# An attention and mixture-of-experts kernel: blocks of one expert's 128 rows become doubles, singles and mixed blocks of two experts' 64 rows each

## The chip, the cores and the metric

The kernel runs on one core of one Trainium2 chip. The metric is the device time of one execution in microseconds (us); shorter is better. All timed runs that are compared here were marked fast, which means within 1.5% of the fastest run of the same kernel; the one single look is named where it comes up.

Trace abbreviations: PE is TensorE (matrix products), PEld its loading of weights, DVE is VectorE, ACT ScalarE, POOL GpSimd and SP SyncE, which here queues the transfers of weights. The granted clock is the share of TensorE's full clock that it was given, 1.00 at most. A "pass" is one matrix-product instruction of the trace; a float32 product shows as two passes, a transpose as one (in the trace of the kernel before a block's layer 1 of 32 products shows 64, its four transposes 4). "L1024" is a line of the kernel file; the changed kernel has other line numbers for the same code.

## The reference, cut to what matters

```python
# attention: 8 batches x 8 heads, 576 tokens, 64 per head, causal, with a bias from s
attn_out = softmax(q k^T / 8 + min(bias, 0)) v           # float32 throughout
x = attn_out -> (8, 576, 512)                            # 4608 tokens

# routing: logits = x @ w_gate (8 experts); local_gate = sigmoid(x @ w_local)
for each token s of a batch, in order:
    fresh_e = argmax(logits[s])
    e = fresh_e if s == 0 or local_gate[s] < 0.5 else e of the token before
    p = softmax(logits[s])
    out[s] = p[e] * (relu(x[s] @ w1[e]) @ w2[e])         # 512 -> 1024 -> 512
```

Each token goes to exactly one expert. With the fixed inputs the eight experts get 573, 516, 565, 575, 717, 459, 513 and 690 tokens. Sorting them by expert and cutting them into blocks leaves partly filled blocks; how many blocks are needed is what the change is about.

## The kernel before

After attention the rows of x are scattered to a buffer ordered by expert. The expert stage then works on blocks of 128 rows of one expert. Four blocks start before the routing is complete ("early"); the others look up their expert and first row in small tables that VectorE computes. A set of one expert's two weight matrices is 4 MB, and the core has three places for such sets.

```python
    def load(i):                                   # set i of weights, eight pieces of 512 KB
        ...
        ws[i] = (wf if wf and i % 3 == 0 else wp).tile([P, DK * F + FK * D], F32, name="w")
        ...
        load_weights(nc, ws[i], w1, w2, j)

    def layer1(i, half):                           # 64 passes per block in all
        ...
        for j in range(4):
            f = slice((g + j) * P, (g + j + 1) * P)
            for c in range(DK):
                mm(ps[:, j, :], lhsT=w[:, c, f], rhs=xT[i][:, c, :], start=(c == 0), stop=(c == DK - 1))
            tick()                                 # hooks: routing, tables, ...
        ...                                        # relu into hT, by VectorE or ScalarE

    def layer2(i):                                 # 16 passes, with 4 transposes in their middle
        ...
        for c in range(FK):
            mm(ps, lhsT=h[:, c, :], rhs=w[:, c, :], start=(c == 0), stop=(c == FK - 1))
            if c == FK // 2 - 1:
                turn_x(i + 2)
            tick()
        ...                                        # times the gate, scattered to the output

    for i in range(NBL):                           # the software pipeline
        if i or not ready:
            load(of[i] + 2)
        layer1(i + 1, 0)
        fetch(i + 3)
        layer1(i + 1, 1)
        layer2(i)
```

A set is requested for each further block, even when the block before had the same expert; only the early blocks share theirs. Behind this list stand conditional passes for more blocks, which these inputs do not enter.

Of the kernel before, what the change touches and what calls it, by code (L numbers as in the profile page):

```python
# [18 lines left out]
P = 128  # L19
# [12 lines left out]
NBLK = N // P + E - 1  # L32
HW = DH + E + 1
X0 = E + 1
XI = H * HW
XW = XI + 2
R = N + 2 * P
EARLY = (0, 0, 1, 1)
SURE = NBLK - 2 - len(EARLY)
# [22 lines left out]
def kernel(  # L62
# [17 lines left out]
    rows_d = nc.dram_tensor("x_rows", (E * R + P, XW), F32, kind="Internal")  # L80
# [12 lines left out]
    with ExitStack() as main:  # L93
        keep = main.enter_context(tc.tile_pool(name="keep", bufs=4))
        wf = main.enter_context(tc.tile_pool(name="wf", bufs=1))
        xs = {}

        def new_x(b):
            xs[b] = keep.tile([P, NB, XW], F32, name="xb")
            return xs[b]  # L100
# [18 lines left out]
        w = wf.tile([P, DK * F + FK * D], F32, name="w")  # L119
# [4 lines left out]
        def fetch_early(bank):  # L124
            for i, e in enumerate(EARLY):
                ready["x"][i] = gx.tile([P, XW], F32, name="xg")
                r0 = e * R + P * EARLY[:i].count(e)
                nc.sync.dma_start(ready["x"][i], rows_d[r0 : r0 + P, :])
# [4 lines left out]
        tail = attention(tc, q, k, vm, s, w_gate, w_local, ident, lg, recs, const, new_x, plan)  # L133
        hooks = [(2, lambda bank: (tail(bank), last.stages[0](bank))), (6, last.stages[1]), (11, last.stages[2]),
                 (13, lambda bank: (last.stages[3](bank), last.stages[4](bank), sort.fill(range(E)), sort.tables())),
                 (14, lambda bank: [f(bank) for f in last.scatters]),
                 (60, lambda bank: in_range(tc, recs, out_of, bank))]
        experts(tc, w1, w2, out, rows_d, ident, sort,
                [("early", e) for e in EARLY] + [("further", i) for i in range(SURE)], hooks, wf, gx, ready)
    total = nc.values_load(sort.total[0:1, 0:1], min_val=0, max_val=NBLK,  # L140
                           skip_runtime_bounds_check_because="a count of blocks")
    with tc.If(total > SURE):
        experts(tc, w1, w2, out, rows_d, ident, sort, [("further", i) for i in range(SURE, SURE + 2)])
        with tc.If(total > SURE + 2):
            experts(tc, w1, w2, out, rows_d, ident, sort, [("further", i) for i in range(SURE + 2, NBLK)])
    wrong = nc.values_load(out_of[0:1, 0:1], min_val=0, max_val=P * NPAIR * 2 * NB,
                           skip_runtime_bounds_check_because="a count of elements")
    with tc.If(wrong > 0):
        attention_general(tc, q, k, vm, vt, s, w_gate, w_local, cum_d, x_d, ident, lg)
        with ExitStack() as again:  # L150
            pool = again.enter_context(tc.tile_pool(name="again", bufs=1))
            ps = again.enter_context(tc.tile_pool(name="again_ps", bufs=3, space=PSUM))

            def bank(n):
                return [ps.tile([P, 512], F32, name="bank") for _ in range(n)]

            sort = Sort(tc, pool, lg, rows_d, ident)
            sort.constants(bank)
            for bs in ((b,) for b in range(B)):
                xs = {b: pool.tile([P, NB, XW], F32, name=f"xb{b % 2}") for b in bs}  # L160
                for b in bs:
                    nc.gpsimd.memset(xs[b], 0.0)
                    for t in range(NB):
                        r0, z = b * S + t * P, min(P, S - t * P)
                        nc.sync.dma_start(xs[b][:z, t, :XI].rearrange("p (a w) -> p a w", w=2 * HW)[:, :, X0 : X0 + P],
                                          x_d[r0 : r0 + z, :].rearrange("p (a w) -> p a w", w=P))
                g = sort.group(bs, xs)
                for f in (*g.stages, *g.scatters):
                    f(bank)
            sort.fill(range(E))  # L170
            sort.tables()
            experts(tc, w1, w2, out, rows_d, ident, sort, [("further", i) for i in range(NBLK)])
# [535 lines left out]
class Sort:  # L708
# [4 lines left out]
    def __init__(self, tc, pool, lg, rows_d, ident):  # L713
        self.tc, self.nc, self.pool, self.lg, self.ident = tc, tc.nc, pool, lg, ident
        self.views = iter(dram_disjoint_views(rows_d[:, :], B * NB + 2 * E + 5))
# [4 lines left out]
    def constants(self, bank):  # L720
# [26 lines left out]
        self.ebi, self.rowi = t("ebi", [P, NBLK], I32), t("rowi", [P, NBLK], I32)  # L747
# [4 lines left out]
        nc.sync.dma_start(next(self.views)[E * R : E * R + P, :], self.empty)  # L752
# [14 lines left out]
    def early(self, bank):  # L767
        for e in sorted(set(EARLY)):
            d, k = slice(e, e + 1), EARLY.count(e)
            self.nc.vector.tensor_tensor(self.done[:, d], self.next[:, d], self.origin[:, d], op=Alu.subtract)  # L770
            self.nc.vector.tensor_scalar(self.done[:, d], self.done[:, d], float(k * P), None, Alu.min)
            self.fill([e], k)

    def tables(self):

        nc, t = self.nc, self.t
        start = t("start", [P, E])
        nc.vector.tensor_tensor(start, self.origin, self.done, op=Alu.add)
        left = t("left", [P, E])
        nc.vector.tensor_tensor(left, self.next, start, op=Alu.subtract)  # L780
        nblk_i = t("nblk_i", [P, E], I32)
        nc.vector.tensor_scalar(nblk_i, left, float(P - 1), None, Alu.add)
        nc.vector.tensor_scalar(nblk_i, nblk_i, 7, None, Alu.logical_shift_right)
        nblk = t("nblk", [P, E])
        nc.vector.tensor_copy(nblk, nblk_i)
        bend = t("bend", [P, E])
        nc.vector.tensor_tensor_scan(bend, self.ones[:, :E], nblk, 0.0, op0=Alu.mult, op1=Alu.add)
        past = t("past", [P, NBLK, E])
        nc.vector.tensor_tensor(past, self.lane[:, :NBLK].unsqueeze(2).to_broadcast([P, NBLK, E]),
                                bend.unsqueeze(1).to_broadcast([P, NBLK, E]), op=Alu.is_ge)  # L790
        eb = t("eb", [P, NBLK])
        nc.vector.tensor_reduce(eb, past, axis=AX, op=Alu.add)
        nc.vector.tensor_scalar(self.ebi, eb, float(E - 1), None, Alu.min)

        nc.vector.tensor_tensor(nblk, bend, nblk, op=Alu.subtract)
        nc.vector.scalar_tensor_tensor(start, nblk, float(-P), start, Alu.mult, Alu.add)
        rise = t("rise", [P, E - 1])
        nc.vector.tensor_tensor(rise, start[:, 1:], start[:, : E - 1], op=Alu.subtract)
        some = [P, NBLK, E - 1]
        part = t("part", some)  # L800
        nc.vector.tensor_tensor(part, past[:, :, : E - 1], rise.unsqueeze(1).to_broadcast(some), op=Alu.mult)
        row = t("row", [P, NBLK])
        nc.vector.tensor_reduce(row, part, axis=AX, op=Alu.add)
        nc.vector.scalar_tensor_tensor(row, self.lane[:, :NBLK], float(P), row, Alu.mult, Alu.add)
        nc.vector.tensor_scalar(row, row, start[:, 0:1], None, Alu.add)

        nc.vector.scalar_tensor_tensor(self.rowi, past[:, :, E - 1], float(E * R), row, Alu.mult, Alu.max)
        nc.vector.tensor_copy(self.total, bend[:, E - 1 : E])
# [131 lines left out]

@with_exitstack
def experts(ctx, tc, w1, w2, out, rows_d, ident, sort, blocks, hooks=(), wf=None, gx=None, ready=None):
# [8 lines left out]
    NBL = len(blocks)  # L951

# [3 lines left out]
    wp = pool("wp", 2 if wf else 3)  # L956
# [7 lines left out]
    ws, xg = (ready["w"], ready["x"]) if ready else ({}, {})  # L964
    at, xT, hT = {}, {}, {}

    sets, of = [], []
    for i, x in enumerate(blocks):
        if not i or x[0] == "further" or x != blocks[i - 1]:
            sets.append(x)  # L970
        of.append(len(sets) - 1)
# [10 lines left out]

    def load(i):
        if i >= len(sets) or i in ws:
            return
        kind, j = sets[i]
        ws[i] = (wf if wf and i % 3 == 0 else wp).tile([P, DK * F + FK * D], F32, name="w")
        if kind == "further":
            j = nc.values_load(sort.ebi[0:1, j : j + 1], engines=[ET.SP], min_val=0, max_val=E - 1,
                               skip_runtime_bounds_check_because="clamped to the experts when it was counted")  # L990
        load_weights(nc, ws[i], w1, w2, j)

    def fetch(i):
        if i >= NBL or i in xg:
            return
        j = blocks[i][1]
        xg[i] = gx.tile([P, XW], F32, name="xg")
        row = nc.values_load(sort.rowi[0:1, j : j + 1], engines=[ET.Pool], min_val=0, max_val=E * R,
                             skip_runtime_bounds_check_because="a block's first row")
        nc.gpsimd.dma_start(xg[i], rows_d[bass.ds(row, P), :])  # L1000
# [12 lines left out]
    def layer1(i, half):  # L1013
# [5 lines left out]
        w = ws[of[i]][:, : DK * F].rearrange("p (c f) -> p c f", c=DK)  # L1019
        ps = ps_h.tile([P, 4, P], F32, name="hp")  # L1020
        for j in range(4):
            f = slice((g + j) * P, (g + j + 1) * P)
            for c in range(DK):
                mm(ps[:, j, :], lhsT=w[:, c, f], rhs=xT[i][:, c, :], start=(c == 0), stop=(c == DK - 1))  # L1024
# [6 lines left out]
    def layer2(i):  # L1031
        ps = ps_y.tile([P, D], F32, name="yp")
        h = hT.pop(i)
        w = ws[of[i]][:, DK * F :].rearrange("p (c d) -> p c d", c=FK)
        for c in range(FK):
            mm(ps, lhsT=h[:, c, :], rhs=w[:, c, :], start=(c == 0), stop=(c == FK - 1))  # L1036
# [9 lines left out]
    load(0)  # L1046
    load(1)
    if not ready:
# [6 lines left out]
    for i in range(NBL):  # L1055
        if i or not ready:
            load(of[i] + 2)
# [41 lines left out]
```

## Time and profile before

| | before |
|---|---|
| time, median of the 3 runs measured first | 918.68 us (918.0 to 919.03) |
| the profiled execution | 908.47 us, span 906.7 us |
| blocks of 128 rows | 41 |
| sets of weights moved | 39 (312 pieces of 512 KB) |
| bytes moved by DMA in all | 230.88 MB |

The profiled execution is 10 us shorter than the timed runs.

From the page of the kernel before: busy time and share of the span by engine, then the rows of TensorE, of its granted clock and of the DMA engines, in tenths over 40 equal slices of the span:

```profile
PE 889.4 (98%) x7239; PEld 652.0 (72%) x7239; DVE 307.6 (34%) x741; ACT 187.5 (21%) x496; POOL 191.1 (21%) x292
...
PE   9999999999999999999999999999999999999994
...
PEclk9999999999999999999999999999999999999998
DMA  9054147455343398698988989898988989898850
```

TensorE is full in nearly every slice, at full clock. The DMA engines are mostly half busy or less in attention and nearly full in the expert stage, the right two thirds of the row. So there are two candidates for a bound in that stage, and the change relieves both.

### The profile page before, as it was taken

Reading aid. Unit: us, or ns where it says so; the run is one execution under the profiler, and the core shown is the slowest. Engines: PE = TensorE matmul, PEld = TensorE weight load, DVE = VectorE, ACT = ScalarE, POOL = GpSimd, SP = SyncE. Lnnn points to the kernel's source line nnn. Section 1 sums busy time; section 2 is a strip of 40 time slices with the busy share of each in tenths; the row PEclk is TensorE's granted clock in tenths of the full one; section 3 lists DMA queues with packets and bytes.
Section 4 is the critical chain, followed back from the end, with each engine's and each line's share of the span. In section 5 each row is a group of like instructions: output and inputs, shape, how many; then the busy total and the mean of one; then the engine's idle time right before and its main releaser. Section 6 shows DMA issues by size and latency. Waiting matters only on the chain.

```text
span 906.7 us, 18152 instructions
## 1 busy us (share of the span) xinstructions
PE 889.4 (98%) x7239; PEld 652.0 (72%) x7239; DVE 307.6 (34%) x741; ACT 187.5 (21%) x496; POOL 191.1 (21%) x292
## 2 busy tenths in 40 slices
PE   9999999999999999999999999999999999999994
PEld 7777767676777967777676767777676777768671
DVE  3666775777776631111111111111111111111110
ACT  5556455555555000000000000000000000000000
POOL 3422345337434051101010110101011010101100
PEclk9999999999999999999999999999999999999998
DMA  9054147455343398698988989898988989898850
GB/s 308 30 174 163 52 145 252 188 166 189 128 134 113 136 319 353 235 342 310 354 294 340 322 323 339 320 348 300 351 324 320 336 321 341 308 353 299 333 202 21
DMA packets 72562, 230.88 MB, mean 255 GB/s; under 512 B 9325, under 2 KB 10637, under 8 KB 72464
## 3 DMA queue, kind: packets, MB, share of 16 engines
q1 hardware_dynamic: 63008, 197.92, 60.8%
q0 software_dynamic: 9312, 31.37, 9.0%
q8 instruction: 61, 1.00, 0.4%
q10 hardware_dynamic: 144, 0.29, 0.1%
q14 instruction: 37, 0.30, 0.1%
HBM read 205.41 MB, written 25.45 MB: 255 GB/s over the span
## 4 chain that ended last, share of the span: by engine, by line
PE 98%; DVE 1%; issue 0%; POOL 0%; POOLq 0%; DVEq 0%
PE hp L1024 32%; PE yp L1036 31%; PE ps L290 11%; PE o L338 11%; PE b L369 4%; PE o L362 4%; PE xp L1007 2%; PE idle L254 1%; DVE r_u L861 0%; DVE r_v L862 0%; PE bank L857 0%; PE bank L872 0%; PE bank L890 0%; PE bank L891 0%; POOL out_dram L1042 0%
## 5 line engine op out<-in xcount | busy, mean ns | idle before, releaser
L1024 PEld LDWEIGHTS hp<-xT,w 128*128 128x128 f32 x2624 | 299.7, 192 | 20.0 <-issue 18.9
L1024 PE MATMUL hp<-xT,w 128*128 128x128 f32 x2624 | 300.9, 275 | 0.8 <-DVE at L1011 0.8
L1036 PE MATMUL yp<-w,hT 128*128 128x512 f32 x656 | 294.6, 592 | 0.0
L1036 PEld LDWEIGHTS yp<-w,hT 128*128 128x128 f32 x656 | 118.5, 190 | 119.1 <-issue 119.1
L296 ACT ACTIVATE sc<-ps,bias 128x320 f32<-128x320 f32 (+4 forms) x448 | 160.7, 467 | 116.8 <-issue 56.4
L1042 POOL DMA_INDIRECT out_dram<-y,at x41 | 40.9, 997 | 493.6 <-DVE y L1041 480.4
L1029 ACT ACTIVATE hT<-hp 128x512 f32<-128x512 f32 x41 | 24.5, 597 | 548.6 <-PE hp L1024 548.6
L1027 DVE TENSOR_SCALAR hT<-hp 128x512 f32<-128x512 f32 x41 | 28.3, 691 | 249.1 <-PE hp L1024 249.1
L290 PE MATMUL ps<-qk 64*128 64x320 f32 (+4 forms) x896 | 109.1, 377 | 3.1 <-DVE r_v L862 2.8
L338 PE MATMUL o<-sc,va 128*64 128x320 f32 (+4 forms) x896 | 100.8, 364 | 0.0
L302 POOL TENSOR_SCALAR_AFFINE_SELECT sc<-sc 128x256 f32<-128x256 f32 (+1 forms) x96 | 59.4, 619 | 149.7 <-ACT sc L296 101.9
L290 PEld LDWEIGHTS ps<-qk 64*128 64x128 f32 x896 | 71.6, 186 | 25.6 <-issue 5.9
L338 PEld LDWEIGHTS o<-sc,va 128*64 128x64 f32 x896 | 56.8, 136 | 42.3 <-issue 18.6
L1041 DVE TENSOR_SCALAR y<-yp,xg 128x512 f32<-128x512 f32 x41 | 30.8, 751 | 115.0 <-PE yp L1036 115.0
L1009 DVE COPY xT<-xp 128x512 f32<-128x512 f32 x41 | 28.4, 691 | 118.3 <-PE xp L1007 118.2
L325 DVE TENSOR_TENSOR sum<-sum,sc 128x640 f32<-128x640 f32 (+2 forms) x96 | 61.5, 641 | 10.1 <-POOL sc L302 5.2
L369 PE MATMUL b<-turn,xT 128*64 128x146 f32 x566 | 50.5, 291 | 0.0
L926 POOL DMA_INDIRECT x_rows<-xb,r_slot_i x40 | 43.7, 1091 | 11.3 <-issue 8.8
L369 PEld LDWEIGHTS b<-turn,xT 128*64 128x64 f32 x566 | 38.6, 137 | 7.8
L362 PE MATMUL o<-one,sum 128*64 128x1 f32 x1024 | 38.3, 197 | 0.0
L382 DVE TENSOR_TENSOR xb<-b,recs 128x292 f32<-128x292 f32 (+1 forms) x94 | 35.4, 404 | 7.7 <-PE b L369 7.6
L362 PEld LDWEIGHTS o<-one,sum 128*64 128x64 f32 x1024 | 35.5, 138 | 0.0
(123 smaller groups left out, 310.7 us busy)
## 6 DMA issues: line engine op xcount, KB each, us to landing
w<-in_w_dram SPq DMA_DIRECT2D x312, 512.0 KB, 9.1
xg<-x_rows POOLq DMA_DIRECT2D x37, 293.0 KB, 8.2
qk<-in_q_dram SPq DMA_DIRECT2D x32, 288.0 KB, 4.8
va<-in_vm_dram SPq DMA_DIRECT2D x35, 256.0 KB, 4.1
qk<-in_k_dram SPq DMA_DIRECT2D x31, 288.0 KB, 5.1
x_rows<-r_empty SPq DMA_DIRECT2D x13, 293.0 KB, 3.8
xg<-x_rows SPq DMA_DIRECT2D x4, 293.0 KB, 5.1
va<-in_vm_dram SPq DMA_DIRECT2D x5, 192.0 KB, 4.1
```

What stands on the lines that cost most here:

```text
L290: mm(ps[:, h, at : at + z - a], lhsT=kb[d, hp, KEYS[c] : KEYS[c] + P], rhs=qb[d, hp, a:z], start=True, stop=True)
L296: nc.scalar.activation(sc[:, h, at : at + z - a], ps[:, h, at : at + z - a], Act.Exp, bias=bias[:, i : i + 1], scale=scale)
L302: nc.gpsimd.affine_select(out=x, in_=x, compare_op=Alu.is_ge, fill=0.0, base=0, pattern=[[0, 2], [0, len(diag)], [1, P]], channel_multipli ...
L325: add(x, x, piece(n, c, 1), op=Alu.add)
L338: mm(o[DH * h : DH * h + DH, a - q0 : z - q0], lhsT=vas[b % 2][:, c, 2 * hp + h, :], rhs=w[:, h], start=(c == 0), stop=(c == (1, NF)[g]))
L362: mm(xs["o", 1][p : p + TL, i : i + 1], lhsT=w, rhs=one, start=True, stop=True)
L369: mm(ps[p : p + TL, t * 2 * HW : (t + 1) * 2 * HW], lhsT=xs["t", g][:, a : a + TL], rhs=w, start=True, stop=True)
L382: nc.vector.tensor_tensor(x, y, rec.unsqueeze(3).to_broadcast([m, k, 2, HW]), op=Alu.mult)
L926: self.s.nc.gpsimd.indirect_dma_start(out=next(self.s.views)[:, :], out_offset=bass.IndirectOffsetOnAxis(ap=self.slot[:z, m : m + 1], axis=0),
L1024: mm(ps[:, j, :], lhsT=w[:, c, f], rhs=xT[i][:, c, :], start=(c == 0), stop=(c == DK - 1))
L1036: mm(ps, lhsT=h[:, c, :], rhs=w[:, c, :], start=(c == 0), stop=(c == FK - 1))
L1042: nc.gpsimd.indirect_dma_start(out=outs[i][:, :], out_offset=bass.IndirectOffsetOnAxis(ap=at[i][:, 0:1], axis=0), in_=y[:, :], element_off ...
```

## The change

The intent is to fill blocks better and to load fewer weights. An expert's rows are now cut into *doubles* (two blocks of 128 that share a set), *singles* (one block) and *halves* (64 rows). Two halves of two experts lie side by side in one *mixed* block, which uses two sets. The lists have fixed lengths, and what a kind cannot use overflows into the next. A fourth place for weights is found by reusing the buffers of x. The tables for all this need more VectorE work, which is spread over nine hooks.

The core of the diff (the table arithmetic, the attention buffers and the rarely taken passes are cut):

```diff
-EARLY = (0, 0, 1, 1)
-SURE = NBLK - 2 - len(EARLY)
+HALF = P // 2
+EARLY = (0, 1)
+WIDTH, SLOTS, MOST = (2 * P, P, HALF), (10, 10, 8), (20, 24, 20)
+ORDER = "DMDSDMSDSDMSDSDMSDSDSDSS"
 ...
-    wp = pool("wp", 2 if wf else 3)
+    wp = pool("wp", 1)
 ...
+    room = {i: ws[i] if i in ws else w3 if i == 3 and ready else wp.tile([P, WS], F32, name=f"w{i}") for i in range(4)}
 ...
     def load(i):
+        for s, (kind, j) in enumerate(sets):
+            if s in ws or s >= 4 and end[s - 4] >= i:
+                continue
+            ws[s] = room[s % 4]
+            e = EARLY[j] if kind == "early" else number(sort.ebi[kinds[kind]], j, ET.SP, E - 1)
+            load_weights(nc, ws[s], w1, w2, e)
 ...  # layer 1
+            if len(w) == 1:
+                for c in range(DK):
+                    mm(ps[:, j, :], lhsT=w[0][:, c, f : f + P], rhs=xT[i][:, c, :], ...)
+            else:
+                for swap in range(2):
+                    for c in range(DK):
+                        for h in range(2):
+                            d = slice(h * HALF, h * HALF + HALF)
+                            n = slice((h ^ swap) * HALF, (h ^ swap) * HALF + HALF)
+                            mm(ps[d, j, n], lhsT=w[h ^ swap][:, c, f + h * HALF : f + h * HALF + HALF],
+                               rhs=xT[i][:, c, n], start=(c == 0), stop=(c == DK - 1))
 ...  # layer 2
+        m = P // len(w)
         for c in range(FK):
-            mm(ps, lhsT=h[:, c, :], rhs=w[:, c, :], ...)
+            for n, wn in enumerate(w):
+                mm(ps[n * m : n * m + m, :], lhsT=h[:, c, n * m : n * m + m], rhs=wn[:, c, :], ...)
             if c == FK // 2 - 1:
                 turn_x(i + 2)
 ...
-            load(of[i] + 2)
+            load(i)
```

In a mixed block, layer 1 is done in tiles of 128 rows by 64 columns of the array, two of which work side by side (in the trace of the kernel before, the paired value products of attention start 6 to 7 ns apart, and a pair of 320 columns repeats every 269 ns); "swap" gives each expert's rows both halves of the 128 hidden units. Layer 2 gives each expert's 64 rows one of the two tiles.

## The prediction

> **What bounds the kernel now.** I began with the page's chain that ended last. It is TensorE almost alone, and two lines of the expert stage carry most of it:
>
> ```profile
> PE 98%; DVE 1%; issue 0%; POOL 0%; POOLq 0%; DVEq 0%
> PE hp L1024 32%; PE yp L1036 31%; PE ps L290 11%; PE o L338 11%; PE b L369 4%; PE o L362 4%; PE xp L1007 2%; PE idle L254 1%; DVE r_u L861 0%; DVE r_v L862 0%; PE bank L857 0%; PE bank L872 0%; PE bank L890 0%; PE bank L891 0%; POOL out_dram L1042 0%
> ```
>
> hp is layer 1, yp layer 2, xp the transposes of a block's rows; the other lines are attention. Next the groups of the two lines, for what TensorE waits for there (last column):
>
> ```profile
> L1024 PE MATMUL hp<-xT,w 128*128 128x128 f32 x2624 | 300.9, 275 | 0.8 <-DVE at L1011 0.8
> L1036 PE MATMUL yp<-w,hT 128*128 128x512 f32 x656 | 294.6, 592 | 0.0
> ```
>
> It waits 0.8 us in 595. So I cut the expert stage by blocks of 128 rows, in the chain in order of time (start, length, what):
>
> ```profile
> 382.62 7.14 PE hp L1024 x64
> 389.77 3.44 PE yp L1036 x8
> 393.20 0.44 PE xp L1007 x4
> 393.64 3.44 PE yp L1036 x8
> 397.08 7.14 PE hp L1024 x64
> ```
>
> A block is 64 + 16 + 4 instructions (a float32 product is two passes, the transposes are one) and repeats every 397.08 - 382.62 = 14.46 us; 34 of them from 382.62 to 874.01 give 14.453. One pass of 128 columns costs 7.14 / 64 = 111.6 ns, one of 512 columns 3.44 / 8 = 430 ns. The mean durations on the page (275, 592) overlap and must not be multiplied. 2624 / 64 = 41 blocks run. Last, the DMA engines in the steady stage (busy us and counts by engine, then clock, DMA share, GB/s):
>
> ```profile
> 400.00:500.00 100.00, 100.00 (x580) 72.88 (x580) 15.36 (x28) 4.18 (x7) 10.18 (x13) 1.00 0.87 326
> ```
>
> TensorE is full at full clock; the DMA engines are 87% busy, close behind, with one 4 MB set of weights per block for most blocks (312 pieces / 8 = 39 sets), but nothing waits on them.
>
> [...] Attention already uses the half-column tiles (128 rows x 64 columns) that mixed blocks will use: the start times of its value products show pairs 6 to 7 ns apart, with a pair of 320 columns repeating every 269 ns, so two tiles run for the price of one. At a change of mode the next start comes some 95 ns later than streaming would give (62 changes from ps to o, mean 92; 48 from b to ps, mean 96), and the first weights are then loaded in the open, another 45 ns (64 columns) to 100 ns (128). [...] with weights of 128 columns the step is 111.6 ns, and in the row sums, which load 64 columns for a product one column wide, it is 58 ns per pair:
>
> ```profile
> 200.27 0.96 PE L362 MATMUL o<-one,sum 128*64 128x1 f32 x28
> 201.09 0.70 PE L369 MATMUL b<-turn,xT 128*64 128x146 f32 x8
> ```
>
> 28 products from 200.27 to 201.09: 29 ns each. [...]
>
> **The change part by part.**
>
> *Fewer blocks.* The main list becomes 4 early blocks (two doubles), then 10 doubles (20 blocks), 10 singles and 4 mixed: 38 instead of 41. I routed the fixed inputs through the reference: experts get 573, 516, 565, 575, 717, 459, 513 and 690 tokens. Before, that is 4 early and exactly 37 further blocks. After, 256 each of the first two experts go early; the rest wants 15 doubles, 1 single and 6 halves. Five doubles too many become 10 singles, one single too many becomes 2 halves: 10, 10 and 8, exactly full. So the conditional passes behind stay unentered. Gain: 3 x 14.45 = 43.4 us, all on TensorE's path.
>
> *Mixed blocks dearer.* Layer 1 becomes 256 passes of 64 x 64 outputs (each half of the rows with its own expert's weights) instead of 64. They alternate between the two column tiles: 128 pairs. A pair loads 64 columns of weights on each tile and streams 64 columns. Loads alone repeat every 58 ns; the last value products, of 64 columns with 64-column weights, were also 55 to 59 ns apart, loads and products overlapped. 128 x 58 = 7.42 us, + 0.3 against 7.14. Layer 2 becomes 32 passes of 512 columns in 16 pairs at about 430 ns: 6.88, as before. Mode changes: into and out of layer 1, into and out of layer 2, and out and back for the transposes in its middle, six. Three into half columns at 95 + 45, three out at 95 + 100: 1.0 us. Together +1.3 per mixed block, 15.8 us; four: +5.4 us.
>
> *Weights.* 2 + 10 + 10 + 8 = 30 sets, not 39: about 38 MB less. As nothing waited for weights, this is worth nothing. Could four places make a new wait? A set is fetched when the set four before it is finished. The tightest place is a double after "mixed, single": one iteration between release and first use, 14.5 us. That is the lead of the old kernel at every block, with no visible wait. Two places freed together by a mixed block have two iterations (29 us) for two sets.
>
> *Tables and start.* The block tables grow to about 86 small VectorE operations, from some 20. At the old ones' pace of 0.20 us from start to start that is about 17 us, now spread over nine hooks. TensorE needs 7.8 us for that stretch, so VectorE falls behind: the first y comes at about 337 us instead of 324.6. It is due only when its PSUM bank is wanted again, two layer 2s later (346 us). The transposed rows of block 2 are queued after three hooks only, ready near 324 as before; the next layer 1 starts at 324.43. Rows of block 4 are the closest:
>
> ```profile
> 339.49 0.61 POOL L1000 DMA_DIRECT2D xg<-x_rows  x1 [7.25 <-DMA x_rows<-xb,r_slot_i]
> ```
>
> They are fetched at 339.5, waiting for the scatter, land 8.2 us later (median), and are wanted at 349.6. GpSimd must now first send the late y, at 338 to 339: the same moment. I allow +0.5 us.
>
> *Attention* keeps its instructions and their order on TensorE; its four x places become slices of one tile, with waits still by slice. 0. The end is one plain block as before: 0.
>
> Sum: 918.7 - 43.4 + 5.4 + 0.5 = 881.2 us.
>
> **Rivals.** (1) *TensorE cannot issue a mixed layer 1 that fast.* 256 loads and 256 products in 7.4 us are 14.5 ns per instruction for 7 us without pause. Against worry: bursts of 96 at 15.6 ns. For it: over 8 us the densest stretch has 295 instructions, 27 ns each[...]. At 27 ns a layer 1 takes 13.9 us: +6.4, four times, makes 907. [...] At 20 ns: 892. (2) *Loads and products of paired tiles do not overlap* when both are 64 wide: 58 + 56 ns per pair, 14.6 us: 910. The few 64-wide pairs seen speak against it. (3) *Weights bind.* The DMA share is 0.87 to 0.90 and the mixed blocks want two sets at once; a late set would cost a few us at up to four places: 885 to 895. Fewer bytes and the unchanged lead speak against. (4) *The start slips,* tables, late y, rows of block 4: the expert stage would be shifted by 2 to 6 us: 883 to 887. (5) *The saved blocks were hidden anyway:* no, TensorE carries the chain alone.
>
> **Range and chances.** The 43.4 us are firm: a count times a steady period. What is uncertain is nearly all in the layer 1 of four blocks: each 1 us there is 4 us. The low end, 876, has cheap mode changes and fewer stalls in noise; the high end, 893, admits 20 ns per instruction or a slipped start. I put 0.14 on rival 1 or 2 taking most of the way to 900, the 2% line. Faster 0.88, same 0.11, slower 0.01.
>
> **What would show it.** In the profile after: hp 3200 times (34 x 64 + 4 x 256), yp 672, xp 152. Plain blocks still 14.45 us apart. In a mixed block 256 hp in about 7.5 us; 13 or more proves rival 1 or 2. TensorE's start at a double after a mixed block, waiting for a DMA of w, would show rival 3. A gap in TensorE between 320 and 350 us shows rival 4. DMA below 0.80 in the expert stage with no gain from it confirms that the weights were hidden. My number is wrong if mixed blocks are far from 15.8 us, or if the lists do not fill as counted and a further pass runs behind.

## The result, and the profile after

| | before | after |
|---|---|---|
| time, median of 4 runs each | 918.86 us (918.0 to 920.03) | 880.22 us (877.01 to 880.61) |
| ratio of the fast runs | | 0.9571 (95%: 0.9546 to 0.9596) |
| span of the profiled execution | 906.7 us | 878.5 us |
| blocks | 41 | 38 |
| weight pieces of 512 KB | 312 | 184 + 56 = 240, so 30 sets |
| DMA in all | 230.88 MB | 192.60 MB |

A ratio here is always the mean time of one kernel's fast runs over that of the other's of the same rounds, so it is not quite the ratio of the medians quoted beside it. The kernel became 38.6 us faster by the medians; 37.5 was predicted.

From the page after, the busy times by engine and the chain that ended last:

```profile
PE 857.3 (98%) x7819; PEld 621.7 (71%) x7819; DVE 311.9 (36%) x796; ACT 185.4 (21%) x493; POOL 187.1 (21%) x290
...
POOL 0%; POOLq 0%
```

The chain is of no use this time: it broke off after the last instructions of GpSimd, and its shares add up to nothing. It does not mean that GpSimd sets the end. The first line shows that TensorE is again busy for 98% of the span, with more instructions than before in less time. Where the chain fails, the groups of TensorE serve, kept apart by shape (count after the x, then busy us, mean ns of one, and what it waited for):

```profile
L1103 PE MATMUL hp<-xT,w 128*128 128x128 f32 x1536 | 178.8, 277 | 3.9 <-issue 3.1 <-DVE at L1089 0.8
...
L1103 PE MATMUL hp<-xT,x 128*128 128x128 f32 x640 | 73.3, 275 | 0.0
L1110 PE MATMUL hp<-xT,w 128*64 128x64 f32 x768 | 31.8, 223 | 0.2
...
L1110 PE MATMUL hp<-xT,x 128*64 128x64 f32 x256 | 15.8, 223 | 0.1
```

A "w" as the last input is one of three places for weights and "x" the fourth, in the storage of x. Plain layer 1 passes: 1536 + 640 = 2176 = 34 x 64. Half-column passes: 768 + 256 = 1024 = 4 x 256. So 34 plain and 4 mixed blocks ran, and no conditional pass. In 4 us of waits no transfer of weights appears.

The steady stage after, in the same view as in the prediction (busy us and counts of PE, PEld, DVE, ACT, POOL, then clock, DMA share, GB/s):

```profile
400.00:500.00 100.00, 99.96 (x772) 70.88 (x772) 15.36 (x28) 4.05 (x7) 11.56 (x15) 1.00 0.78 266
```

TensorE is as full as before. The DMA engines fell from 0.87 to 0.78.

The next view is TensorE in order of time, from a second measurement of the changed kernel (the run after_again below). Columns: start, length with modelled end, what, count. Lengths overlap (674.50 + 3.60 lies past 678.03), so only differences of starts count:

```profile
674.50 3.60 PE L1125 MATMUL yp<-x,hT 128*128 128x512 f32 x8
678.03 7.69 PE L1110 MATMUL hp<-xT,w 128*64 128x64 f32 x256
685.64 3.70 PE L1125 MATMUL yp<-x,hT 128*128 128x512 f32 x8
689.18 0.60 PE L1085 MATMUL xp<-ident,xg 128*128 128x128 f32 x4
689.62 3.60 PE L1125 MATMUL yp<-x,hT 128*128 128x512 f32 x8
693.05 7.31 PE L1103 MATMUL hp<-xT,w 128*128 128x128 f32 x64
700.29 3.65 PE L1125 MATMUL yp<-w,hT 128*64 128x512 f32 x16
703.87 0.66 PE L1085 MATMUL xp<-ident,xg 128*128 128x128 f32 x4
704.46 3.65 PE L1125 MATMUL yp<-w,hT 128*64 128x512 f32 x16
708.04 7.41 PE L1103 MATMUL hp<-xT,x 128*128 128x128 f32 x64
```

A mixed layer 1 begins at 678.03 and what follows it at 685.64: 7.61 us for 256 passes, where a plain one takes 7.14. Its layer 2 runs from 700.29 to 708.04: 7.75 us where a plain one (685.64 to 693.05 is such, but with one mode change before it) takes 7.31 or 7.32. The plain pieces next to a mixed one cost about 0.10 us more: 678.03 - 674.50 = 3.53 against 3.44, 689.18 - 685.64 = 3.54 against 3.44, 700.29 - 693.05 = 7.24 against 7.14. With another 0.11 in the layer 1 after it, this mixed block costs 0.09 + 0.47 + 0.10 + 0.10 + 0.43 + 0.11 = 1.30 us more than a plain one. The second to fourth mixed blocks of this run average 1.31.

### The profile page after: what moved, and what is told of

The parts are those of the page before. It is cut to its first block, busy times and chain, and to the rows that moved or that the text cites.

```text
span 878.5 us, 19221 instructions
## 1 busy us (share of the span) xinstructions
PE 857.3 (98%) x7819; PEld 621.7 (71%) x7819; DVE 311.9 (36%) x796; ACT 185.4 (21%) x493; POOL 187.1 (21%) x290
## 2 busy tenths in 40 slices
DMA packets 61926, 192.60 MB, mean 219 GB/s; under 512 B 7965, under 2 KB 9277, under 8 KB 61824
## 5 line engine op out<-in xcount | busy, mean ns | idle before, releaser
L1125 PE MATMUL yp<-w,hT 128*128 128x512 f32 (+1 forms) x480 | 201.7, 594 | 0.0
L1103 PEld LDWEIGHTS hp<-xT,w 128*128 128x128 f32 x1536 | 176.9, 193 | 16.0 <-issue 14.9
L1103 PE MATMUL hp<-xT,w 128*128 128x128 f32 x1536 | 178.8, 277 | 3.9 <-issue 3.1
L1132 POOL DMA_INDIRECT out_dram<-y,at x38 | 38.5, 1013 | 473.4 <-DVE y L1131 439.7
L1125 PEld LDWEIGHTS yp<-w,hT 128*128 128x128 f32 (+1 forms) x480 | 77.8, 180 | 81.6 <-issue 80.4
L1125 PE MATMUL yp<-x,hT 128*128 128x512 f32 (+1 forms) x192 | 86.8, 595 | 0.0
L1103 PEld LDWEIGHTS hp<-xT,x 128*128 128x128 f32 x640 | 72.9, 192 | 5.4 <-issue 5.4
L1103 PE MATMUL hp<-xT,x 128*128 128x128 f32 x640 | 73.3, 275 | 0.0
L1125 PEld LDWEIGHTS yp<-x,hT 128*128 128x128 f32 (+1 forms) x192 | 32.9, 181 | 32.5 <-issue 32.3
L975 POOL DMA_INDIRECT x_rows<-x,r_slot_i x40 | 43.2, 1079 | 11.4 <-issue 8.8
```

Source lines behind the costliest of these rows:

```text
L975: self.s.nc.gpsimd.indirect_dma_start(out=next(self.s.views)[:, :], out_offset=bass.IndirectOffsetOnAxis(ap=self.slot[:z, m : m + 1], axis=0),
L1103: mm(ps[:, j, :], lhsT=w[0][:, c, f : f + P], rhs=xT[i][:, c, :], start=(c == 0), stop=(c == DK - 1))
L1125: mm(ps[n * m : n * m + m, :], lhsT=h[:, c, n * m : n * m + m], rhs=wn[:, c, :], start=(c == 0), stop=(c == FK - 1))
L1132: nc.gpsimd.indirect_dma_start(out=outs[i][:, :], out_offset=bass.IndirectOffsetOnAxis(ap=at[i][:, 0:1], axis=0), in_=y[:, :], element_off ...
```

## The experiments

My theory: TensorE carries the expert stage alone. Three blocks fewer are worth 43.4 us, four mixed blocks cost some 5 us of it, and the saved transfers are worth nothing. (Of the fourth place I came to expect that it is needed; three_places tests it.) The main rival: fewer bytes, or more places for weights, gave part of the gain, and mixed blocks cost more than they seem to. Second rival: the start of the stage moved. Twelve runs were made in three calls, each call on one chip; a call's kernels are compared with each other and with the kernel before on the same chip.

### First call: what each part is worth

**before_again and after_again** are the two kernels unchanged.

> The kernel before, unchanged, run again with a profile. Why: its recorded profile has a span of 906.7 us, its timed runs 918 to 920, while the changed kernel's timed runs (877.0 to 880.6) agree with its profile (878.5). In the changed kernel's profile all sequencers crawl for 3 to 5 us at three places (TensorE stands 2.1 us at 337, and then runs at half clock for 3.4 us), 9.5 us in all; the kernel before shows none in its one profile. Theory A (these crawls strike both kernels, run by run): timed runs 915 to 920, ratio 1.00, and a profile of a span above 910 shows such crawls. Theory B (the change brings them): a profile free of them at 906 to 908, and the 10 us between span and timed run come from elsewhere.

> The changed kernel, unchanged, with a second profile. Theory A: ratio 0.957, and the crawls are at other places or of another size than in the first profile. Theory B: the crawl at the start of the expert stage (332 to 337 us from the start, in the new table operations) is there again at the same place, with 4 to 5 us.

Measured: before_again 908.71 us (ratio 1.0), after_again 871.21 us, ratio 0.9591 (0.9573 to 0.9608). This chip runs both kernels faster than the first measurement did: by 10 us before and by 9 us after. The step between the kernels is 37.3 us by the medians of the same rounds (908.48 to 871.21), 37.4 by the spans (907.2 to 869.8). Neither trace has a stretch in which the instruction streams crawl, as both expectations call it (from 330 to 340 us TensorE is busy for 10.00 of 10 us in both), and on this chip timed runs and profile agree; the third call takes this up.

**mixed_plain** gives a mixed block the first set only, through the plain passes. Its result is wrong (relative error 0.215): half of the rows in mixed blocks get the other expert's weights. All transfers, places and tables stay.

```diff
-        w = [ws[s][:, : DK * F].rearrange("p (c f) -> p c f", c=DK) for s in of[i]]
+        w = [ws[s][:, : DK * F].rearrange("p (c f) -> p c f", c=DK) for s in of[i][:1]]
 ...
-        w = [ws[s][:, DK * F :].rearrange("p (c d) -> p c d", c=FK) for s in of[i]]
+        w = [ws[s][:, DK * F :].rearrange("p (c d) -> p c d", c=FK) for s in of[i][:1]]
```

> Wrong result on purpose: the four mixed blocks still fetch both halves and both experts' weights, but both layers are computed for all 128 rows with the first expert's weights, in full tiles like a plain block. It takes away the half-column tiles alone. My theory (a mixed block costs 1.3 to 1.6 us more than a plain one): 5 to 6.5 us less than the changed kernel, about 874. Rival (the half tiles do not overlap well, or the instruction stream starves them, somewhere the trace does not show): 15 us or more less. Rival (mixed blocks cost through their two sets of weights): no change.

Measured: 864.61 us, ratio 0.9519 (0.9503 to 0.9535). The mean is 6.7 us below that of after_again, the span 7.3 us. Four blocks at 1.31 make 5.2; the rest is one stop in the first mixed layer 1 of after_again, whose PE lines in order of time read (brackets: idle before, and what ended it):

```profile
390.02 0.22 PE L1110 MATMUL hp<-xT,x 128*64 128x64 f32 x1
391.92 0.22 PE L1110 MATMUL hp<-xT,w 128*64 128x64 f32 x1 [1.69 <-issue]
```

For 1.90 us no product starts, and no semaphore is waited for ("issue"). What held TensorE up there is not shown. The stop belongs to a place of the kernel: it lies after pass 235 of the 256, and in the first mixed block of three later traces there is a gap after the same pass, of 0.34 us (after_control), 0.85 us (fewer_switches) and 0.28 us (three_places). Only its size differs, and in four other traces it is absent. With the stop, 5.2 + 1.9 = 7.1 us are accounted for. mixed_plain also tests the first term: it has 38 plain-like blocks in place of 41, and lies 44 us below the kernel before (mean 864.8 against 908.7), where 3 x 14.45 = 43.4 was worked out. Its trace is sharper: from the start of the sixth layer 1 to that of the last, 462.48 us against 505.84 in before_again, which is 43.36 less.

**doubles_only** keeps shared weights, four places and the new tables, but has no mixed blocks: 4 early blocks, 10 doubles and 17 singles are 41 blocks again, with 29 sets of weights. It is correct.

```diff
-WIDTH, SLOTS, MOST = (2 * P, P, HALF), (10, 10, 8), (20, 24, 20)
-ORDER = "DMDSDMSDSDMSDSDMSDSDSDSS"
+WIDTH, SLOTS, MOST = (2 * P, P, HALF), (10, 17, 0), (20, 24, 20)
+ORDER = "DSSDSSDSSDSSDSSDSSDSSDSDSDS"
 ...
-        ts(n_i, left, float(HALF - 1), None, Alu.add)
+        ts(n_i, left, float(P - 1), None, Alu.add)
 ...
-            ts(n[i], left, float(HALF if i == 1 else 0), None, Alu.is_gt)
+            ts(n[i], left, 0.0, None, Alu.is_gt)
```

> Correct result. No mixed blocks: the rest of every expert is cut into 10 doubles and 17 singles, 41 blocks as before, with 29 sets of weights instead of 39, four places, and the new tables. It does the sharing of weights alone. My theory (weights were hidden, only the count of blocks counts): ratio 1.00 to the kernel before, within 0.5%, with the DMA share in the expert stage down to some 0.7. Rival (less weight traffic itself speeds TensorE or takes waits away): 0.98 or less.

Measured: 909.01 us, ratio 1.0003 (0.9986 to 1.002). In the stretches of its steady stage:

```profile
400.00:500.00 100.00, 100.00 (x580) 72.88 (x580) 14.64 (x28) 4.18 (x7) 10.88 (x14) 1.00 0.79 276
```

The DMA share fell as in the changed kernel (to 0.71 to 0.75 in the three stretches of 100 us after this one), TensorE issued the same 580 passes in 100 us as before, and nothing was gained. From the start of the sixth layer 1 to that of the last it is 505.84 us, in before_again and here alike. Sharing weights is worth nothing in time, and the larger tables cost nothing on this chip. The rival of bytes falls.

### Second call: mode changes and places

This call ran on another chip, on which the kernel before takes 919.37 us. **after_control** is the changed kernel.

> The changed kernel unchanged, on the same chip as the three runs beside it, as their standard; ratio to the kernel before 0.957 to 0.960. A third profile for the start of the expert stage and for the 1.9 us in which TensorE stood in the first mixed block's layer 1 of the second profile (there while the DMA share was 0.93): if it stands there again at about the same place, it is of the kernel and not of chance.

Measured: 878.09 us, ratio 0.9551 (0.9523 to 0.9579), mean 878.18.

**more_switches** spreads the four transposes in a mixed layer 2 over four places. The trace shows each as a full-width product (128*128) between half-column ones (128*64), so there are four excursions instead of one: six more mode changes per mixed block, 24 in all.

```diff
-            if c == FK // 2 - 1:
+            if c == FK // 2 - 1 and len(w) == 1:
                 turn_x(i + 2)
+            if len(w) == 2 and FK // 2 - 2 <= c < FK - 2:
+                turn_x(i + 2, (c - FK // 2 + 2,))        # one of the four transposes
```

> Correct result. In the layer 2 of a mixed block the four transposes are put one by one after four of the eight products instead of together: six more changes of tiling mode per mixed block, 24 in all, and nothing else. [...] 24 x 0.165 = +4.0 us to the changed kernel, 0.5%. Rival (the extra time of mixed blocks is in the paired products, changes are nearly free): no difference.

**fewer_switches** does a mixed block's transposes before its layer 2, where TensorE is in full-width mode anyway (128*128, in the layer 1 before): two mode changes fewer per mixed block, 8 in all.

```diff
+        if len(w) == 2:
+            turn_x(i + 2)
         for c in range(FK):
 ...
-            if c == FK // 2 - 1:
+            if c == FK // 2 - 1 and len(w) == 1:
                 turn_x(i + 2)
```

> Correct result. The transposes of a mixed block's iteration stand ahead of its layer 2 instead of in its middle: two changes of mode fewer per mixed block, 8 in all: 8 x 0.165 = -1.3 us, 0.15%. In the trace the mixed layer 2 runs through its 32 products without a break. Rival (changes nearly free, or transposes ahead of layer 2 uncover a wait of theirs): 0 or slower.

Measured: more_switches 881.3 us, mean 881.46, so +3.3 us over after_control; fewer_switches 876.85 us, mean 876.72, so -1.5 us. The order is as expected, the sizes roughly: 3.3 / 24 = 0.14 us and 1.5 / 8 = 0.18 us per change, against the 0.165 that I had worked with: some 0.095 us until the next start, and 0.045 to 0.1 us more for the first weights. (The starts around the mixed blocks in the first profile of the changed kernel show starts that are 0.09 to 0.10 us later, and then 0.05 us more where weights of 64 columns or the transposes follow and 0.10 us where a plain layer 1 or 2, with weights of 128 columns, does.) But the four runs of after_control alone spread over 3.7 us, more than either step, and the three intervals overlap, so the times prove little. The traces show the cost directly; first more_switches, then fewer_switches (PE in order of time):

```profile
502.85 2.80 PE L1131 MATMUL yp<-w,hT 128*64 128x512 f32 x12
505.57 0.33 PE L1089 MATMUL xp<-ident,xg 128*128 128x128 f32 x1
505.83 1.08 PE L1131 MATMUL yp<-w,hT 128*64 128x512 f32 x4
506.84 0.33 PE L1089 MATMUL xp<-ident,xg 128*128 128x128 f32 x1
...
511.51 0.71 PE L1109 MATMUL hp<-xT,x 128*128 128x128 f32 x4
```

```profile
492.73 7.31 PE L1103 MATMUL hp<-xT,w 128*128 128x128 f32 x64
...
500.40 7.09 PE L1127 MATMUL yp<-w,hT 128*64 128x512 f32 x32
507.42 7.41 PE L1103 MATMUL hp<-xT,x 128*128 128x128 f32 x64
```

Four half-column passes, two pairs of 430 ns, would take 0.86 us from start to start without a change; they take 1.01 (505.83 to 506.84). A transposition, 0.11 us in a plain block, takes 0.26 (505.57 to 505.83). Both differences, 0.15 us, are the price of one mode change. The whole agrees: from the layer 1 before a mixed layer 2 to the next layer 1 it is 14.99 us in the changed kernel (693.05 to 708.04 above), 15.90 in more_switches and 14.69 in fewer_switches (492.73 to 507.42), within 0.01 us in all four mixed blocks of each. That is +0.91 us for six changes and -0.30 for two.

**three_places** takes the fourth place for weights away.

```diff
-    room = {i: ... for i in range(4)}
+    room = {i: ... for i in range(3 if ready else 4)}
 ...
-            if s in ws or s >= 4 and end[s - 4] >= i:
+            if s in ws or s >= len(room) and end[s - len(room)] >= i:
 ...
-            ws[s] = room[s % 4]
+            ws[s] = room[s % len(room)]
```

> Correct result. Three places for weights in the main list instead of four, all else as in the changed kernel. By my reading a set may start to load once the set three before it is done; directly after each mixed block, and in three cases for the second set after it, its layer 1 then follows at once, so TensorE waits for 2 MB: seven waits of 6 to 9 us, 42 to 63 us, slower than the kernel before (910 to 935). Rival (four places are a reserve that is not needed, since weights were hidden with three before): within 5 us of the changed kernel.

Measured: 879.18 us, ratio 0.9563 (0.9533 to 0.9592), mean 0.8 us above after_control, within the scatter. TensorE is as full as with four:

```profile
400.00:500.00 100.00, 99.99 (x776) 71.15 (x775) 14.92 (x28) 4.18 (x7) 11.57 (x15) 1.00 0.78 268
```

My expectation fell. Its error was about when a place is free. I had counted it as free when a block's layer 2 has ended, and a load as issued where it stands in the program. But the queue of weight transfers runs ahead of the program and stops at each piece on its own (88 waits for TensorE's expert stage for 30 sets in three_places). The queue's own waits show it; first the kernel before, then three_places (what waited for what: us in total, times, longest us):

```profile
SPq L938 <- PE yp L1036: 321.6, 36, 16.8
```

```profile
SPq L987 <- PE yp L1125: 251.1, 76, 15.5
...
SPq L987 <- PE hp L1103: 34.2, 12, 5.8
```

In the kernel before (the trace of before_again), the weights that wait for TensorE's expert stage wait only for layer 2s, 36 times for 39 sets, which fits a place that comes free as a whole. In three_places there are 88 such waits for 30 sets, and 12 of them end with a layer 1. So the half of a place that holds the first matrix is free when layer 1 of its last block has ended, the other half after layer 2. In the tightest place of three_places (a set two blocks after the last use of the same place) each half then has some 7.3 + 14.5 = 21.8 us until it is needed (an estimate from the times of layer 2 and of a block); a half is 2 MB, which at the 268 GB/s of the stretch above is some 8 us (an estimate). None of TensorE's waits in this trace is for a transfer. The fourth place was not needed for speed.

### Third call: the time of the chips, and the layout of mixed blocks

A third chip, on which the kernel before takes 919.38 us. **before_profile** is a single look at the kernel before, to have its trace on a chip of the slower kind; **after_control2** is the changed kernel again.

> The kernel before with a third profile. On two of the three chips so far it took 917 to 920 us and on one 908; the changed kernel's profiles on the slow two show sequencers that crawl at fixed places of the attention stage and the start of the expert stage, and none on the fast one. If the crawl belongs to the chip and not to the change, then on a chip where the kernel before takes 917 or more its profile shows TensorE standing 0.6 to 2 us in several places of its attention stage too; on one where it takes 908, none.

> The changed kernel unchanged, on the same chip as the runs beside it, as the standard for the half per cent in question. 0.955 to 0.960 of the kernel before.

Measured: before_profile 920.03 us (one run, so its state is marked unknown), span 918.3; after_control2 879.0 us, ratio 0.9563 (0.9537 to 0.9588), mean 879.05. Here is TensorE in before_profile in order of time, then the same stretch as a sum, for before_profile and for before_again:

```profile
329.83 3.96 PE L1024 MATMUL hp<-xT,w 128*128 128x128 f32 x34
334.49 0.27 PE L1024 MATMUL hp<-xT,w 128*128 128x128 f32 x1 [0.70 <-issue]
...
336.63 0.27 PE L1024 MATMUL hp<-xT,w 128*128 128x128 f32 x1 [1.05 <-issue]
338.05 0.37 PE L1024 MATMUL hp<-xT,w 128*128 128x128 f32 x1 [1.15 <-issue]
```

```profile
330.00:340.00 10.00, 6.32 (x44) 5.54 (x44) 0.00 (x0) 0.60 (x1) 5.23 (x6) 0.84 1.04 301
```

```profile
330.00:340.00 10.00, 10.00 (x46) 6.12 (x45) 1.80 (x4) 0.00 (x0) 2.18 (x3) 1.00 1.04 347
```

In the middle of a layer 1, TensorE stops several times without waiting for anything that the trace shows, and its granted clock drops (0.84 in this stretch). On the fast chip the same stretch is full. Such crawls come at about 143 to 149, 220 to 230 and 332 to 343 us, in both kernels, in every trace of the second and third calls and in the first profile of the changed kernel; on the chip of the first call they are absent in both kernels. In them TensorE stops, VectorE's table operations stand up to 1.15 us apart where 0.03 is usual (after_control), and single register instructions of SyncE take up to 0.70 us (0.03 to 0.05 elsewhere); GpSimd's scatters of rows keep their step of some 1.3 us. They begin near the end of the three batches of ten scatters; two batches of five, at 244 to 251 and 281 to 288 us, have none. Why some chips crawl and one does not stays open.

They explain all of the difference between before_profile and before_again: the fourth layer 1 begins at 350.52 us against 339.44, 11.1 us later, and from the sixth to the last layer 1 both take 505.84 us. The first profile of the kernel before shows no crawl either. Since none of the 16 timed runs of this kernel on the two slower chips is below 917 us, that profile (908.47 us) was probably taken on another chip than the timed runs.

**mixed_full_tile** computes a mixed layer 1 without half columns: full 128-column weights of each expert, with only that expert's 64 rows streamed. That is 128 passes, and no mode change in layer 1.

```diff
-                for swap in range(2):
+                for h in range(2):
+                    n = slice(h * HALF, h * HALF + HALF)
                     for c in range(DK):
-                        for h in range(2):
-                            d = slice(h * HALF, h * HALF + HALF)
-                            n = slice((h ^ swap) * HALF, (h ^ swap) * HALF + HALF)
-                            mm(ps[d, j, n], lhsT=w[h ^ swap][:, c, f + h * HALF : f + h * HALF + HALF],
-                               rhs=xT[i][:, c, n], start=(c == 0), stop=(c == DK - 1))
+                        mm(ps[:, j, n], lhsT=w[h][:, c, f : f + P], rhs=xT[i][:, c, n],
+                           start=(c == 0), stop=(c == DK - 1))
```

> Correct result. The layer 1 of mixed blocks with full tiles: for either half of the rows all 128 columns of its expert's weights, 128 passes with 64 columns streamed, instead of 256 passes in pairs of half tiles. A pass is then bound by the load of 128 columns of weights, 111.6 ns: 128 x 0.1116 = 14.3 us instead of 7.6, two changes of mode fewer (-0.3): +6.4 us per mixed block, +25 us to the changed kernel, about 0.985 of the kernel before. Rival (only products count, loads hide: 128 passes of 64 columns at 56 ns = 7.2 us): no slower than the changed kernel.

Measured: 904.77 us, ratio 0.9844 (0.9815 to 0.9873), correct; the mean is 25.5 us above after_control2. One such layer 1 and the start of what follows (PE in order of time):

```profile
485.66 14.40 PE L1108 MATMUL hp<-xT,w 128*128 128x64 f32 x128
499.90 3.65 PE L1123 MATMUL yp<-x,hT 128*128 128x512 f32 x8
```

499.90 - 485.66 = 14.24 us for 128 passes, 111 ns each. Here a pass of 64 columns with weights of 128 columns takes as long as one of 128 columns, 111.6 ns in a plain layer 1: loading weights sets the pace in this layer 1, not the product. (The 56 ns of the expected rival is half of 111.6, an estimate.) Half-column tiles are what makes mixed blocks pay. Without them three blocks fewer are worth only 14.6 us (919.38 to 904.77) of their 43.

**mixed_together** keeps TensorE in half columns from a mixed block's layer 1 into its layer 2, by doing the layer 2 of the block before first. This drops four of the six mode changes, and the transposes come after layer 2.

```diff
     for i in range(NBL):
         ...
+        first = len(of[i]) == 2 or i + 1 < NBL and len(of[i + 1]) == 2
+        if first:
+            fetch(i + 3)
+            layer2(i)
         layer1(i + 1, 0)
-        fetch(i + 3)
+        if not first:
+            fetch(i + 3)
         layer1(i + 1, 1)
-        layer2(i)
+        if not first:
+            layer2(i)
```

(The mixed block's transposes are also moved behind its layer 2.)

> Correct result; meant to beat both kernels. Around a mixed block the order is layer 2 of the block before, layer 1 and layer 2 of the mixed block, then its transposes and layer 1 of the next block: two changes of tiling mode per mixed block instead of six, 16 fewer in all: 16 x 0.165 = -2.6 us to the changed kernel (0.3%), if layer 2 needn't wait for the second half of layer 1's result (it is needed 3.4 us later and takes 0.7 us to move). Rival: that wait, or the later layer 1 behind it, shows up and eats the gain: 0 or slower.

Measured: 877.6 us, ratio 0.9537 (0.9513 to 0.956), correct; mean 876.99, that is 2.1 us below after_control2. The trace has the intended order (PE in order of time):

```profile
484.54 3.60 PE L1125 MATMUL yp<-x,hT 128*128 128x512 f32 x8
488.07 8.00 PE L1110 MATMUL hp<-xT,w 128*64 128x64 f32 x255
...
495.97 7.03 PE L1125 MATMUL yp<-w,hT 128*64 128x512 f32 x31
502.93 0.66 PE L1085 MATMUL xp<-ident,xg 128*128 128x128 f32 x4
```

It beats the kernel before clearly. Against the changed kernel the two intervals overlap, so the times alone do not settle a gain. The traces agree with one: from the sixth layer 1 to the last it takes 467.13 us, in after_control2 469.24. Around a mixed block four steps from layer 1 to layer 1 take 58.8 us against 59.4 to 59.6, some 0.6 to 0.8 less; only the first, with a stop of 0.70 us, gains nothing. The layer 1 here, 488.07 to about 495.9, shows one thing more: on the slower chips a mixed layer 1 takes 7.8 to 8.7 us, where the fast chip takes 7.61. In each of them, 28 in seven traces, lies one gap of 0.22 to 0.35 us between passes 72 and 76, and the longest have a second one after pass 215 or 235. So the first gap too belongs to a place of the kernel, and the fast chip does not show it.

## Why the prediction was right

*What bounds the kernel.* The prediction said that TensorE carries the expert stage alone. doubles_only shows it: the DMA share fell much as in the change, and the ratio is 1.0003. "The saved blocks were hidden anyway" falls with mixed_plain.

*Fewer blocks, -43.4 us.* Counts and lists came out as worked out, and the step from the kernel before to mixed_plain is -44 us.

*Mixed blocks, +1.3 us each.* (Four of them are 5.1 to 5.2 us; the prediction's own sum has 5.4.) Measured: 1.31 us on the fast chip, from the starts of instructions. The parts agree too. Of layer 1's 0.47, 0.28 is the pace of the pairs, which repeat every 58 ns as foreseen; the rest of the extra time, 1.02 us, is six mode changes where 1.0 was worked out. What this term lacked is time that no repeating pattern shows: one stop of 1.9 us in the first mixed layer 1 of after_again, and on the slower chips 0.2 us or more in each. There the four blocks cost 6.8 us (the first profile of the changed kernel, after_control2) to 7.5 us (after_control). This is a small piece of rival 1. Its large form fell: TensorE took 256 loads and 256 products in 7.61 us. Rival 2, loads and products of paired tiles that do not overlap, fell with the same number; mixed_full_tile shows what a layer 1 of 128 passes costs when each loads 128 columns of weights, 14.24 us.

*Weights, 0.* Right in its result. But the reason given was in part a misreading: "The tightest place is a double after "mixed, single": one iteration between release and first use, 14.5 us" treats a place as released as a whole, as in the kernel before. In the changed kernel it comes free by pieces (10 waits of the queue end with a layer 1 in after_again, 12 in three_places), and the lead is longer. The misreading did no harm in the prediction, and much harm in what I expected of three_places.

*Tables and start, +0.5.* Half right. On the fast chip the first output is sent by GpSimd at 338.23 us, "at 338 to 339" as predicted, and TensorE still runs without a stop from 311 to 347 us. There the term is 0. On the slower chips TensorE does stand there, but so it does in the kernel before, and for longer; rival 4 did not come about.

*The end, 0.* Missed: from the start of the last layer 1 to the end of the span it is 32.77 us in before_again and 31.61 in after_again, 1.2 less, all of it after TensorE's last pass, in closing branches and semaphores. No run tests why.

*The sum.* On the fast chip, -43.4 + 5.2 + 1.9 - 1.2 = -37.5 us; the spans differ by -37.4. On the two slower chips of the experiments the step is larger, -41.3 and -40.4 us by the medians, and in the first measurement -38.6. The traces of the third call say where: -43.4 for the blocks, +6.8 for the mixed ones, -0.9 at the end and -3.3 in the crawls are -40.8, and the spans differ by -40.7 (before_profile to after_control2). The crawls cost the kernel before more, above all in its third layer 1: the step to the fourth takes 21.58 us there against 19.67, where 14.45 is usual. Part of it is the clock: it stays at half for 6.8 us in before_profile and for 3.4 in after_control2, some 1.7 us of difference (an estimate). This part varies from trace to trace: in fewer_switches the clock does not drop there, in mixed_together, the same up to that point, it stays at half for 6.8 us too. Why the kernel before is hit more in its timed runs as well is not settled. So the closeness of 881.2 to 880.22 owes something to chance: mixed blocks that were dearer than predicted, an end that was shorter, and an unknown crawl nearly cancel.

## What to carry to other kernels

First find which of two nearly full resources carries the time, and price the change in units of that one: here a count of blocks times a steady period was nearly the whole answer, and 38 MB less traffic was worth nothing. Half-column tiles let two half-filled blocks of different weights share one block's time here at a cost of some 9% of it (1.31 of 14.45 us): 256 loads and 256 products took 7.61 us in half columns, and 128 passes with weights of 128 columns 14.24 us. Before you count on, or pay for, another buffer, look at what exactly a transfer waits for: here a place that is released by halves had a lead of some 21.8 us (an estimate) where I had counted on none.
